# A delta-rule attention with a feed-forward layer: units of four batches, O on four corners, and the first chunk's inverse in halves

## The chip, the cores and the metric

The kernel runs on one core of a Trainium2 chip. The metric is device time in microseconds. Five engines work beside one another, each through its own instructions in order: TensorE (PE; its weight loads are listed as PEld), VectorE (DVE), ScalarE (ACT), GpSimd (POOL) and SyncE (SP), which here issues nearly all DMAs. The kernel before took 265.98 us, the median of three runs (265.12 to 269.84).

## The reference: what is computed

There are 4 batches, 8 heads, 768 tokens and 48 elements per head. For each batch and head, with k normalised:

```
for t in range(S):
    y[:, :, t] = q[t] @ state
    v_old = k_n[t] @ state
    state = state + beta[t] * outer(k_n[t], v[t] - v_old)
```

y is put together as x (3072 tokens by 384), and the feed-forward layer gives `gelu_tanh(x @ w_in) @ w_out`, with w_in 384x2048 and w_out 2048x384. All inputs and the output are float32; the products are made in bf16.

## The kernel before

**Chunks and units.** The 768 tokens are cut into 12 chunks of 64. One chunk of all 32 (batch, head) pairs is two *units* (u = 2c + x). The 128 partitions hold two halves a of 64 tokens. The loads (L458) put batches 2a + x, x = 0 and 1, side by side into the free dimension of half a. Unit x is batch x of each half, with all 8 heads. A head has a slot 2g + p; p says in which 64 rows of the transposed k and q it lies, and g is one of four.

**What a unit does (`prep`).** k is normalised (`sq`, `sum`, `pow`, `eps`, `inv`, then `kn`, L510), times -beta (`kb`, L512), q is copied (`qb`). The twelve 128x128 pieces of k, kb and q are transposed: for units 0 to 5 on PE (`T`, L520, evicted as `kT`), from unit 6 on by a DMA that SP issues (`turn`, L523). `G2` (L542) and `G` (L534) are the products of k with kb, and of kb with k and q; DVE copies them under triangular masks (`ln`, L546; `wp`, L552). A 64x64 triangular inverse per head follows, five rounds of two products with an eviction after each: A, then `rt` on DVE (2 times the identity is added), then B, then `xi` or `bde` on ACT or DVE. For units 0 and 1 the products are on 64x64 corners of the array (`At`, `Bt`, L567), for later ones on block-diagonal 128x128 weights (L596), which POOL and ACT fill.

**What a chunk does (`chain`).** With the state: K (L642) and `R` (subtract v), `U` or `Um` (the inverse applied, L665) and `Un`, S (L675) and `Sn` (the next state), Q (also L642) and O (L689) into one pair of PSUM banks, `On` copies that out into `xo`. In K, Q and S the four 64x64 corners of the array are taken in turn. In O the row half and the column half are the same a, so two corners are used:

```
for p in range(2):
    for a in range(2):
        ins = e.matmul(at("O", P, hf(a), p, x, g), wp[ss[x]][hf(a), 4 * p + g, C:2 * C], ub[hf(a), x, p, g, :], ...)
```

`xo` is transposed to xT: chunks 0, 1 and 11 on PE (`X`, L710, evicted as `xT`), the others by a DMA (`turnx`, L702).

**The feed-forward part (`mlp`).** For one chunk (256 rows): 16 `up` steps of three products (L731), `gelu` on ACT, two blocks of four `down` steps (L743), `Z` (eviction) and the stores (L754), two per block, one for each half a. w_in and w_out are loaded by POOL (`w1`, L466; `w2`, L470).

**The order.** The order on every engine is written out by hand in `ORDER`, and the PSUM bank of every product in `BANKS`; waits follow from the data and the banks. An item such as `up.3.5/0` is the first `up` at position 3.5. `fill` (L428) is a product of zeros that PE runs while it would wait otherwise; there are 71. On SP the order has loads, `turn`, `turnx` and stores in one queue, so that an item that waits holds those behind it.

Of the kernel before, what the change touches and what calls it, by code (L numbers as in the profile page):

```python
# [18 lines left out]
        fill/0 fill/1 fill/2 fill/3 fill/4 fill/5 fill/6 fill/7 fill/8 fill/9 fill/10 fill/11 fill/12 fill/13 fill/14 betaT.-28/0  # L19
        fill/15 fill/16 fill/17 fill/18 fill/19 fill/20 fill/21 fill/22 fill/23 fill/24 fill/25 T.0/0 fill/26 fill/27 T.1/0 G2.0/0  # L20
        G.0/0 fill/28 fill/29 fill/30 fill/31 fill/32 G2.1/0 G.1/0 At.0/0 fill/33 fill/34 fill/35 fill/36 Bt.0/0 fill/37 At.1/0
        fill/38 At.0/1 fill/39 Bt.1/0 fill/40 Bt.0/1 fill/41 fill/42 At.1/1 fill/43 At.0/2 fill/44 Bt.1/1 fill/45 Bt.0/2 fill/46
        At.1/2 At.0/3 T.2/0 Bt.0/3 T.3/0 Bt.1/2 At.0/4 G2.2/0 fill/47 fill/48 G.2/0 G2.3/0 At.1/3 fill/49 fill/50 fill/51 Bt.1/3
        fill/52 fill/53 fill/54 fill/55 At.1/4 Bt.0/4 fill/56 Bt.1/4 fill/57 A.2/0 G.3/0 fill/58 fill/59 B.2/0 U.0.5/0 T.4/0 fill/60
        fill/61 O.0.7/0 A.2/1 G.4/0 fill/62 fill/63 X.0.8/0 B.2/1 A.3/0 fill/64 fill/65 fill/66 up.3.5/0 A.2/2 B.3/0 up.3.5/1 B.2/2
        up.3.5/2 fill/67 up.3.5/3 up.3.25/0 A.3/1 S.0.5/0 up.3.25/1 B.3/1 up.3.25/2 K.2.5/0 up.3.25/3 up.3/0 fill/68 up.3/1 A16.2/0
        G2.4/0 up.3/2 A.3/2 up.3/3 B.2/3 up.3.75/0 fill/69 up.3.75/1 B.3/2 up.3.75/2 A.4/0 up.3.75/3 A16.3/0 fill/70 B.4/0 A32.2/0
        B.3/3 T.5/0 A.4/1 B.2/4 down.4.5/0 B.4/1 down.4.54/0 A32.3/0 down.4.58/0 B.3/4 down.4.62/0 A.4/2 Um.2.5/0 G2.5/0 G.5/0 Q.2.6/0
        S.2.5/0 O.2.7/0 down.4/0 B.4/2 down.4.04/0 A.5/0 down.4.08/0 X.2.8/0 B.5/0 down.4.12/0 up.5.75/0 up.5.25/0 A.5/1 up.5.25/1
        A16.4/0 up.5.25/2 B.5/1 up.5.75/1 up.5.25/3 up.5.75/2 A.5/2 up.5.75/3 K.4.5/0 up.5/0 B.4/3 B.5/2 up.5/1 G2.6/0 G.6/0 up.5/2  # L30
        A32.4/0 up.5.5/0 up.5/3 up.5.5/1 up.5.5/2 A16.5/0 up.5.5/3 B.4/4 A.6/0 B.5/3 down.6.5/0 B.6/0 down.6.54/0 A32.5/0 G2.8/0
        G2.7/0 A.6/1 B.5/4 down.6.58/0 G.8/0 down.6.62/0 Um.4.5/0 B.6/1 Q.4.6/0 G.7/0 O.4.7/0 G2.9/0 A.6/2 A.8/0 down.6/0 A.7/0 B.6/2
        G.9/0 B.8/0 down.6.04/0 B.7/0 down.6.08/0 A.9/0 A16.6/0 A.8/1 down.6.12/0 A.7/1 B.9/0 B.8/1 up.7.25/0 B.7/1 up.7.25/1 B.6/3
        up.7/0 up.7.25/2 up.7/1 up.7.25/3 A32.6/0 up.7/2 A.7/2 up.7/3 A.9/1 A.8/2 S.4.5/0 up.7.5/0 B.9/1 up.7.5/1 B.7/2 up.7.75/0
        up.7.5/2 up.7.75/1 up.7.5/3 up.7.75/2 A16.7/0 up.7.75/3 A.9/2 K.6.5/0 B.7/3 B.6/4 B.8/2 B.9/2 down.8/0 A32.7/0 down.8.04/0
        B.7/4 down.8.08/0 A16.8/0 down.8.12/0 Um.6.5/0 B.8/3 Q.6.6/0 G2.10/0 O.6.7/0 G.10/0 A16.9/0 down.8.5/0 G2.11/0 S.6.5/0 G.11/0
        down.8.54/0 down.8.58/0 B.9/3 A32.8/0 A.10/0 down.8.62/0 K.8.5/0 B.10/0 B.8/4 up.9.75/0 up.9.25/0 up.9.75/1 up.9.25/1
        up.9.75/2 A.10/1 up.9.75/3 A32.9/0 up.9.25/2 A.11/0 B.10/1 up.9.25/3 up.9.5/0 B.9/4 up.9.5/1 G2.13/0 up.9.5/2 up.9.5/3 G.13/0
        Um.8.5/0 Q.8.6/0 B.11/0 A.10/2 G.12/0 G2.12/0 O.8.7/0 A.13/0 B.10/2 up.9/0 up.9/1 B.13/0 A.11/1 up.9/2 A16.10/0 up.9/3 A.12/0
        B.11/1 A.13/1 S.8.5/0 B.10/3 B.13/1 B.12/0 A.11/2 down.10/0 A.12/1 down.10.04/0 B.11/2 down.10.08/0 up.11.75/0 B.12/1  # L40
        up.11.75/1 A.13/2 up.11.75/2 up.11/0 up.11.75/3 B.13/2 up.11/1 A.12/2 A32.10/0 up.11/2 up.11.25/0 up.11/3 up.11.25/1 A16.11/0
        up.11.25/2 B.12/2 up.11.25/3 up.11.5/0 B.11/3 down.10.12/0 up.11.5/1 K.10.5/0 B.10/4 up.11.5/2 A32.11/0 A16.13/0 up.11.5/3
        down.10.5/0 B.11/4 A16.12/0 down.10.54/0 B.13/3 B.12/3 down.10.58/0 Um.10.5/0 down.10.62/0 G2.14/0 Q.10.6/0 S.10.5/0 O.10.7/0
        G.14/0 A32.13/0 down.12/0 A32.12/0 down.12.5/0 B.13/4 down.12.04/0 A.14/0 down.12.08/0 G2.15/0 G.15/0 K.12.5/0 down.12.54/0
        B.12/4 down.12.12/0 B.14/0 down.12.58/0 Um.12.5/0 down.12.62/0 up.13.75/0 Q.12.6/0 G2.17/0 O.12.7/0 G.17/0 up.13.75/1 A.15/0
        up.13.75/2 up.13/0 A.14/1 up.13/1 up.13.75/3 up.13/2 up.13.5/0 up.13/3 up.13.5/1 B.15/0 up.13.5/2 B.14/1 up.13.5/3 up.13.25/0
        G.16/0 G2.16/0 up.13.25/1 up.15.5/0 up.13.25/2 S.12.5/0 up.13.25/3 up.15.5/1 A.15/1 up.15.5/2 A.16/0 A.14/2 up.15.5/3 A.17/0
        B.15/1 down.14/0 B.16/0 B.14/2 down.14.04/0 B.17/0 A.16/1 down.14.08/0 A.15/2 down.14.12/0 A.17/1 B.16/1 up.15/0 B.15/2
        up.15/1 B.17/1 up.15/2 A16.14/0 A16.15/0 up.15/3 up.15.25/0 A.16/2 up.15.25/1 B.14/3 up.15.25/2 A.17/2 up.15.25/3 B.15/3
        B.16/2 K.14.5/0 A32.14/0 up.15.75/0 B.17/2 up.15.75/1 G2.18/0 up.15.75/2 A16.16/0 up.15.75/3 A32.15/0 A16.17/0 B.14/4 B.16/3  # L50
        B.15/4 down.16/0 G.18/0 G2.19/0 down.14.5/0 Um.14.5/0 down.14.54/0 B.17/3 down.16.04/0 S.14.5/0 G.19/0 Q.14.6/0 down.14.58/0
        down.16.08/0 A.19/0 A.18/0 O.14.7/0 K.16.5/0 down.14.62/0 A32.17/0 B.18/0 B.19/0 down.16.12/0 down.16.5/0 B.17/4 A.18/1
        A32.16/0 down.16.54/0 A.19/1 down.16.58/0 B.18/1 G2.20/0 G.20/0 B.16/4 down.16.62/0 up.17.5/0 B.19/1 up.17.5/1 Um.16.5/0
        up.17.5/2 A.20/0 up.17.5/3 up.17.75/0 G2.21/0 up.17.75/1 B.20/0 up.17.75/2 up.17.25/0 up.17.75/3 up.17.25/1 A.19/2 up.17.25/2
# [12 lines left out]
        up.25.25/3 down.24.04/0 down.24.5/0 down.24.08/0 up.25/0 up.25.5/0 up.25/1 down.24.12/0 up.25/2 down.24.54/0 up.25/3
        down.24.58/0 up.25.5/1 down.24.62/0 down.26/0 up.25.5/2 down.26.5/0 up.25.5/3 down.26.54/0 down.26.04/0 down.26.58/0
        down.26.08/0 down.26.62/0 down.26.12/0
    """,  # L70
    "act": """
        loadk.-40/0 tmpl.-11/0 beta.-24.5/0 pow.0/0 triw.-3/0 ladj16.-0.2/0 ladj16.0.8/0 pow.1/0 tri.-5/0 ladj32.0.8/0 tri.-7/0
# [237 lines left out]
def bass_deltanet__then__act_gelu_tanh_kernel(  # L310
# [13 lines left out]
    NU = 2 * NC  # L324
    DIRECT = lambda u: (2, 3, 4, 5) if u < 8 else (2, 4)
    GROUPS = [[c] for c in range(NC)]
    TURN, TURNX, TILED = 6, 2, 2

    F = Flow()
    A = F.add  # L330

    with nc.allow_non_contiguous_dma("strided loads"), nc.allow_low_precision("bf16 pipeline"):
# [39 lines left out]
        def hf(a, n=C):  # L372
            return slice(64 * a, 64 * a + n)
# [437 lines left out]
```

## Time and profile before

| | |
|---|---|
| median of three runs | 265.98 us (265.12 to 269.84) |
| profiled execution | 266.2 us |
| its span in the profile | 264.4 us |
| clock granted to PE | 1.00 |
| chain that ended last | PE 78%, DVE 7%, DMA 5%, rest under 3% each |
| first product of the feed-forward part | starts at 39.35 us |
| last product of PE | ends at about 260.6 us |
| last O | starts at 238.54 us |

The profile is of one execution. A group line gives the source line, the engine, the operation, out<-in with shapes, the count, the busy time, the mean duration of one, and the engine's idle time before it with what ended it. Instructions of one engine overlap, so that the time from the start of one to the start of the next is often less than its duration.

### The profile page before, as it was taken

The numbers are of one execution on the slowest core, as the hardware profiler recorded it, in microseconds if no ns is written. First come the engines' busy times: TensorE is split into PE (matmuls) and PEld (weight loads), VectorE is DVE, ScalarE is ACT, GpSimd is POOL, SyncE is SP. The second block draws the span as 40 slices with busy tenths as digits, with TensorE's granted clock in tenths as the row PEclk, the third lists the DMA queues.
The fourth block names the chain that finished last, engine by engine and source line by source line (L and its number), as shares of the span: only waits on it lengthen the run. The fifth ranks groups of instructions, "written<-read, shape, count | busy, mean of one in ns | idle before, by whom it ended". The sixth has DMA issues, their size and how long they took to land.

```text
span 264.4 us, 12466 instructions
## 1 busy us (share of the span) xinstructions
PE 253.8 (96%) x5629; PEld 191.6 (72%) x5629; DVE 202.0 (76%) x317; ACT 174.8 (66%) x264; POOL 144.5 (55%) x220
## 2 busy tenths in 40 slices
PE   7899998999899999999999999999999999999994
PEld 2557566877677876877886888877888878778762
DVE  8899796978899999899779888889886876551000
ACT  3758676777886894498663468935788657556431
POOL 8633698849899889875855674480635222110000
PEclk9999999999999999999999999999999999999999
DMA  5996999999999999948997589238149064044023
GB/s 105 175 154 124 146 204 193 177 134 151 158 164 155 141 162 137 188 88 165 169 173 100 125 165 147 48 81 144 25 63 180 5 133 82 2 35 101 6 47 72
DMA packets 117908, 31.86 MB, mean 120 GB/s; under 512 B 111968, under 2 KB 117088, under 8 KB 117856
## 3 DMA queue, kind: packets, MB, share of 16 engines
q1 hardware_dynamic: 113968, 27.63, 69.7%
q0 software_dynamic: 2880, 3.15, 7.6%
q8 instruction: 44, 0.72, 1.2%
q10 hardware_dynamic: 1008, 0.30, 0.5%
q14 instruction: 8, 0.07, 0.1%
HBM read 20.64 MB, written 4.72 MB: 96 GB/s over the span
## 4 chain that ended last, share of the span: by engine, by line
PE 78%; DVE 7%; DMA 5%; ACT 2%; SPq 2%; issue 2%; POOL 2%; POOLq 0%; ACTq 0%
PE ps L743 23%; PE ps L731 21%; PE ps L596 18%; DMA W<-in_moe_w_in_dram 4%; PE ps L428 3%; PE ps L567 3%; PE ps L642 2%; DMA kraw<-in_k_dram 2%; DVE ln L546 2%; PE ps L689 2%; SPq L523 2%; PE ps L534 2%; PE ps L665 1%; DVE rt L603 1%; PE ps L542 1%
## 5 line engine op out<-in xcount | busy, mean ns | idle before, releaser
L731 PE MATMUL ps<-xT,W 128*128 128x256 bf16 x576 | 82.4, 273 | 0.8 <-DMA W<-in_moe_w_in_dram 0.7
L376 ACT ACTIVATE bd<-ps 64x512 bf16<-64x512 f32 x111 | 64.5, 589 | 18.0 <-PE ps L596 16.0
L743 PE MATMUL ps<-W,gT 128*128 128x384 bf16 x384 | 76.3, 326 | 0.0
L736 ACT ACTIVATE gT<-ps 128x1024 bf16<-128x1024 f32 x48 | 48.4, 1021 | 27.0 <-PE ps L731 26.6
L731 PEld LDWEIGHTS ps<-xT,W 128*128 128x128 bf16 x576 | 48.7, 98 | 9.5 <-DMA W<-in_moe_w_in_dram 1.0
L603 DVE TENSOR_TENSOR rt<-ps,two 128x512 bf16<-128x512 f32 x66 | 44.2, 687 | 10.6 <-PE ps L596 9.9
L590 POOL COPY bd<-xi 64x256 f32<-64x256 f32 x64 | 25.1, 394 | 42.4 <-ACT xi L376 30.2
L743 PEld LDWEIGHTS ps<-W,gT 128*128 128x128 bf16 x384 | 32.3, 97 | 15.0 <-ACT gT L736 0.2
L586 POOL TENSOR_SCALAR_AFFINE_SELECT bd<-ln 64x512 bf16<-64x512 bf16 x44 | 28.9, 658 | 22.5 <-DVE ln L546 18.4
L376 DVE CAST bd<-ps 64x512 bf16<-64x512 f32 x45 | 30.8, 686 | 5.1 <-PE ps L596 3.9
L552 DVE CAST_PREDICATED wp<-mup,ps 128x1024 bf16<-128x1024 uint16 (+1 forms) x26 | 29.3, 1133 | 2.3 <-PE ps L534 2.3
L489 POOL TENSOR_TENSOR nrm<-nrm,half 128x16 f32<-128x16 f32 x9 | 26.3, 2929 | 2.1 <-DVE nrm L486 1.9
L376 ACT ACTIVATE xi<-ps 128x512 bf16<-128x512 f32 x31 | 18.3, 594 | 12.1 <-PE ps L596 6.9
L596 PE MATMUL ps<-rt,bd 128*128 128x64 bf16 x528 | 25.5, 194 | 0.3 <-DVE rt L603 0.2
L596 PE MATMUL ps<-wp,bd 128*128 128x64 bf16 (+1 forms) x528 | 24.7, 188 | 1.0 <-issue 0.5
L596 PEld LDWEIGHTS ps<-wp,bd 128*128 128x128 bf16 x528 | 21.3, 97 | 5.5 <-issue 1.1
L596 PEld LDWEIGHTS ps<-rt,bd 128*128 128x128 bf16 x528 | 21.1, 98 | 5.0 <-DVE rt L603 2.4
L603 DVE TENSOR_TENSOR rl<-ps,two 128x384 bf16<-128x384 f32 (+1 forms) x44 | 20.8, 485 | 4.8 <-PE ps L596 4.4
L428 PE MATMUL ps<-wz 128*128 128x512 bf16 x71 | 21.8, 413 | 1.3 <-DVE wz L382 1.2
L510 POOL TENSOR_TENSOR tok<-kraw,nrm 128x384 bf16<-128x384 f32 x21 | 17.6, 841 | 8.4 <-DVE nrm L493 8.1
L546 DVE CAST_PREDICATED ln<-mlo,ps 128x512 bf16<-128x512 uint16 x24 | 16.5, 687 | 4.9 <-PE ps L542 4.6
L512 POOL TENSOR_TENSOR tok<-tok,bsb 128x384 bf16<-128x384 bf16 x21 | 17.5, 836 | 2.7 <-DVE tok L510 1.9
(98 smaller groups left out, 334.5 us busy)
## 6 DMA issues: line engine op xcount, KB each, us to landing
qraw<-in_q_dram SPq DMA_DIRECT2D x24, 192.0 KB, 5.1
vraw<-in_v_dram SPq DMA_DIRECT2D x24, 192.0 KB, 4.9
out_dram<-ob SPq DMA_DIRECT2D x47, 96.0 KB, 2.6
kraw<-in_k_dram SPq DMA_DIRECT2D x22, 192.0 KB, 5.3
W<-in_moe_w_in_dram POOLq DMA_DIRECT2D x2, 768.0 KB, 9.2
W<-in_moe_w_out_dram POOLq DMA_DIRECT2D x2, 768.0 KB, 10.8
kraw<-in_k_dram SPq DMA_DIRECT2D x3, 96.0 KB, 4.0
kT<-tok SPq DMA_TRANSPOSE x18, 5.0
```

Of the source, the lines that this page charges most:

```text
L376: return e.activation(out, in_, ACT.Copy) if e is nc.scalar else e.tensor_copy(out, in_)
L428: return e.matmul(P(f"fill{i}")[:, :], wz[:, 0:128], wz[:, 0:512])
L489: e.tensor_tensor(nr[:, 1, hx], nr[:, 0, hx], half[:, hx], ALU.pow),
L546: A("dve", z + "ln", lambda e, P: e.copy_predicated(ln[m][:, :, :].rearrange("p (x g) t -> p x g t", x=2), mlo[:, :].bitcast(U16).unsqueez ...
L552: A("dve", z + ("wp" if nh == 2 else "wph"), lambda e, P, cs=cs, nh=nh: e.copy_predicated(wp[s][:, :, cs], mup[:, cs].bitcast(U16).unsquee ...
L586: A("pool", z + "X1", lambda e, P, src=src, dst=dst: e.affine_select(out=dst, in_=src, compare_op=ALU.not_equal, fill=1.0, base=0, pattern ...
L590: A("pool", z + "bdc", lambda e, P, src=src, dst=dst: e.tensor_copy(dst.bitcast(F32), src.bitcast(F32)), reads=[w("xi")], writes=[n(f"bd{a ...
L596: ins = e.matmul(P(name)[:, C * h + lo:C * h + C], bd[s][:, h, :], rhs[:, h, lo:C])
L603: A("dve", z + f"rt{lo or str()}", lambda e, P, i=i, lo=lo, r_=r_: e.tensor_tensor(r_[:, :, lo:C], P(ps(f"A{i}")).rearrange("p (h t) -> p ...
L731: ins = e.matmul(P(ph)[:, w * f:w * f + w].rearrange("p (x t) -> p x t", x=2), W1[:, j, 128 * (i + f):128 * (i + f) + 128], x_[:, :, j, :] ...
L736: A("act", z + "gelu", lambda e, P, i=i, ph=ph: e.activation(g_[:, i:i + nf, 0:w], P(ph).rearrange("p (f t) -> p f t", f=nf), ACT.Gelu_app ...
L743: ins = e.matmul(P(po)[:, 0:DM], g_[:, f, 128 * b:128 * b + 128], W2[:, f, :], start=(f == 0), stop=(f == FC - 1))
```

## The change

**Layout.** The loads put batches 2a + p side by side, and unit x takes every second of the 16 columns (p, head): the heads 2g + x of all four batches. p, which was the parity of the head, is now the batch within the half. The state, `rs` and `xo` are ordered g before x, so that the 384 columns of a token are consecutive; `R` and `On` copy without a permutation.

**O and Q.** Both write PSUM rows of half a ^ p in place of a, so that O's four products per g are on four corners. A token's half in `xo` is then a ^ p. For block 0 (p = 0) the halves are in order and both are stored by one DMA (`outw`); block 1 has two stores with the halves exchanged.

**First chunk.** For units 0 and 1 the inverse is made for four head slots at a time (`Ath`, `Bth`, `rth`, `xih`; five rounds as before). Transposes and G of q are split off (`Tq`, `Gh`, evicted by `qT`, `wph`), so that k goes ahead. U, O, X and their evictions of chunk 0 are done for each unit (x) by itself, X for each block.

**Other.** Chunk 1's xT is made by a DMA (`TURNX` 1 in place of 2). The table of the square root is loaded at ACT's start (`tmpl` waits for it). `ORDER` and `BANKS` are new throughout: 68 `fill` in place of 71; on SP the first `turnx` stands after chunk 5's k loads and ahead of one q load, chunk 2's v loads and the `turn` of units 7 and 8.

The core of the diff:

```diff
-    TURN, TURNX, TILED = 6, 2, 2
+    TURN, TURNX, TILED, SPLIT = 6, 1, 2, 2
...
-                view = {"k": k, "q": q, "v": v}[n].rearrange("(a x) h (c t) d -> a c t (x h) d", a=2, t=C)
+                view = {"k": k, "q": q, "v": v}[n].rearrange("(a p) h (c t) d -> a c t (p h) d", a=2, t=C)
...
-            kr, qr = (raw[y][r][:, H * x:H * x + H, :] for y in "kq")
+            kr, qr = (raw[y][r][:, x::2, :].rearrange("t (p g) d -> t p g d", p=2) for y in "kq")
...
+                for ys, tn in (((0, 1), "T"), ((2,), "Tq")) if u < SPLIT else (((0, 1, 2), "T"),):
...
+            for gn, rhs in (("G", (0,)), ("Gq", (2,))) if u < SPLIT else (("G", (0, 2)),):
...
+                        A("pe", z + "Ath", lambda e, P, pa=pa, con=con, lo=lo, f=product: f(e, P, pa, con, lo), ...
+                          alloc=(pa, 1), mode="t", mm=H, pos=u)
+                        A("dve", z + f"rt{lo or str()}h", lambda e, P, pa=pa, lo=lo, r_=r_, y=y: e.tensor_tensor(
+                            r_[:, hs[y], lo:C], P(pa)[:, 0:4 * C].rearrange("p (h t) -> p h t", h=4)[:, :, lo:C],
...
-                o = 512 * b + 4 * D * x + D * g
-                return P(ps(name))[r, o:o + D]
+                o = 512 * b + 2 * D * g + D * x
+                return P(ps(name) if name != "O" or not first else ps(f"O{x}"))[r, o:o + D]
...
-                        ins = e.matmul(at(name, P, hf(a), p, x, g), kT[ss[x]][hf(p, D), y, g, hf(a)], so[hf(p, D), a, x, g, :],
+                        ins = e.matmul(at(name, P, hf(a ^ p if y else a), p, x, g), kT[ss[x]][hf(p, D), y, g, hf(a)], so[hf(p, D), a, g, x, :],
...
-                    for p in range(2):
-                        for a in range(2):
-                            ins = e.matmul(at("O", P, hf(a), p, x, g), wp[ss[x]][hf(a), 4 * p + g, C:2 * C], ub[hf(a), x, p, g, :],
+                    for p, a in quad if x in xs else ():
+                        ins = e.matmul(at("O", P, hf(a ^ p), p, x, g), wp[ss[x]][hf(a), 4 * p + g, C:2 * C], ub[hf(a), x, p, g, :],
...
-                for a in range(2):
-                    r0 = (2 * a + b % 2) * S + C * g[b // 2]
-                    A("act" if final and a else "sp", z + "out", lambda e, P, a=a, r0=r0, o_=o_: e.dma_start(out[r0:r0 + C, :], o_[hf(a), :]),
+                rows = out.rearrange("(a p c t) m -> p c a t m", a=2, p=2, t=C)[b % 2, g[b // 2]]
+                for a in (0, 1) if b % 2 else (slice(0, 2),):
```

More of the change, by code (lines that the diff above doesn't have):

```diff
@@ L149 @@
+        out.26.5/0 outw.26/0
     """,
@@ L410, in preset @@
                 A("pool", "0tmplz", lambda e, P: e.memset(tmpl[:, C:2 * C], 0.0), writes=["tmplz"], pos=-11)
-                A("act", "0tmpl", lambda e, P: e.activation(tmpl[:, 0:C], two[:, :], ACT.Copy, scale=-0.5), reads=["two"],
+                A("act", "0tmpl", lambda e, P: e.activation(tmpl[:, 0:C], two[:, :], ACT.Copy, scale=-0.5), reads=["two", "one"],
                   writes=["tmpl"], pos=-11)
@@ L561, in prep @@
+            if u < TILED:
+                hs = [slice(4 * y, 4 * y + 4) for y in range(2)]
+                for y, _, k_ in halves:
+                    A(("dve", "pool"), z + "X1h", lambda e, P, y=y: e.tensor_tensor(
+                        xi[m][:, hs[y], :], ln[m][:, hs[y], :], two[:, :].unsqueeze(1).to_broadcast([128, 4, C]), ALU.add), reads=[w("ln") + k_, w("ln"), "two"],
+                      writes=[w("xi") + k_], pos=u)
                 for i in range(1, 6):
                     con, conn = (wp[s][:, :, 0:C], n("wp")) if i % 2 else (ln[m], w("ln"))
[L564 to L568 removed]
@@ L720, in mlp @@
             w = 256 * len(g)
[L721 removed]
+            x_, xn = xT[gi % NX], [f"xT{gi % NX}.{256 * i}{k_}" for i in range(len(g)) for k_ in "ab"]
             g_, gn = gT[gi % NG], f"gT{gi % NG}"
```

456 lines of the change are left out of this document (244 added, 212 removed), and 17 rows, old and new, of the table BANKS.

## The prediction

> **What bounds the kernel now.** I read the page's busy shares and clock first, then the busy times by stretch, then TensorE's groups by form, and last the timeline around the first chunk.
>
> ```profile
> PE 253.8 (96%) x5629; PEld 191.6 (72%) x5629; DVE 202.0 (76%) x317; ACT 174.8 (66%) x264; POOL 144.5 (55%) x220
> ...
> PEclk9999999999999999999999999999999999999999
> ```
>
> TensorE (PE) is busy 96% of the span at full clock. No other engine comes near that on average, but the stretches say more (columns: stretch, length, then PE, PEld, DVE, ACT, POOL, clock, DMA share, GB/s):
>
> ```profile
> 30.00:40.00 10.00, 9.94 (x231) 6.41 (x230) 8.53 (x12) 7.11 (x12) 8.77 (x10) 1.00 1.09 186
> ...
> 60.00:80.00 20.00, 18.93 (x458) 14.59 (x455) 18.01 (x30) 16.27 (x25) 18.02 (x19) 1.00 1.22 159
> 80.00:100.00 20.00, 19.78 (x416) 15.86 (x414) 19.25 (x30) 16.37 (x27) 17.86 (x20) 1.00 1.16 146
> 100.00:120.00 20.00, 19.07 (x562) 15.24 (x560) 18.54 (x30) 12.95 (x20) 16.12 (x27) 1.00 0.94 142
> ...
> 140.00:160.00 20.00, 20.00 (x463) 15.38 (x460) 17.72 (x24) 10.23 (x15) 12.11 (x21) 1.00 0.85 142
> ```
>
> From 60 us on PE misses only 1 us in 20, and from 140 us nothing: an instruction less on PE there ends the kernel earlier, as long as its order always has something ready. DVE and POOL are nearly as full between 60 and 120 us. Before 40 us "busy" misleads, because PE runs fillers (products of zeros, L428) while it waits:
>
> ```profile
> L428 PE MATMUL ps<-wz 128*128 128x512 bf16 x71 | 21.8, 413 | 1.3 <-DVE wz L382 1.2
> ...
> L642 PE MATMUL ps<-st,kT 48*64 48x48 bf16 x704 | 9.7, 189 | 0.0
> ...
> L689 PE MATMUL ps<-us,wp 64*64 64x48 bf16 x384 | 8.3, 187 | 0.3
> ...
> L675 PE MATMUL ps<-us,tok 64*64 64x48 bf16 x352 | 4.8, 188 | 0.2 <-ACT us L376 0.2
> ```
>
> Of the 71 fillers 67 start before 39.35 us, where the first product of the feed-forward part (`up`, L731) starts. The other three groups have 48 columns each and one instruction lasts 187 to 189 ns in all of them, but 32 of L689 (the O step) take 8.3/12 = 0.69 us and 32 of L675 (the S step) 4.8/11 = 0.44 us. The timeline shows the same:
>
> ```profile
> 15.43 0.44 PE L567 MATMUL ps<-wp,xi 64*64 64x64 bf16 x16 [0.25 <-POOL xi L558]
> ...
> 35.88 0.69 PE L689 MATMUL ps<-us,wp 64*64 64x48 bf16 x32
> ...
> 39.35 0.24 PEld L731 LDWEIGHTS ps<-xT,W 128*128 128x128 bf16 x3 [0.53 <-issue]
> ...
> 43.59 0.44 PE L675 MATMUL ps<-us,tok 64*64 64x48 bf16 x32
> ```
>
> Start to start that is (0.69-0.19)/31 = 16 ns for O and 8 ns for S. O uses two corners of the array (row half a with column half a), S and the K and Q products (L642) use four. L567, on two corners with 64 columns, also shows 16 ns: about 33 ns for a corner in every case.
>
> **The change, part by part.**
>
> *O on four corners.* Same 32 instructions. Nearest rows: L675 on four corners below (0.44 us), L689 itself above (0.69 us). I take 0.44, since L642 and L675, with different row orders, both give it: 0.25 us for each O, 11 of them in the stretch that PE bounds: -2.75 us (bounds 0 and -2.75). The twelfth lies in the head and is counted there. Q stays on four corners: 0. What becomes late instead: nothing, O ends in an eviction (On) that only gains from an earlier start.
>
> What speaks against it: in K and S each row half keeps a bank of its own, in the new O both row halves write both banks, and no row has that on four corners. The nearest is L567, whose two row halves write one bank: its products start 16 ns apart, while 64 columns take 27 ns (three of L731's 256 columns take 0.33 us). They overlap in the shared bank.
>
> The Trainium skill, page "TensorEngine Tiling (Array Packing)", section "Gotcha 1: PSUM Pressure", says that different row tiles cannot access one PSUM bank at the same time. By that rule the new O would stay at 0.69 us, and the sum would be -1.05 in place of -3.8 us. The trace does not agree with it, by the 16 ns against 27 ns of L567.
>
> *The head.* I add up what PE must issue before the first `up`, by its order. Prices from rows: filler 0.214 us (0.427 for the first ones), twelve transposes 0.67, G2 0.22, G 0.27, an A or B product of a unit 0.235, one of the first two units 0.33, U 0.58, O 0.58 or 0.3, X 0.33. Before: 15 fillers end at 6.48 us; then beta's transposes 0.86, 52 fillers 11.1, five T 3.35, four G2 0.88, five G 1.35, twenty At and Bt 6.6, five A or B 1.2, U, O and X 1.5: 33.3 us. It starts at 39.35, so 6.0 us are gaps: 0.66 for beta and 5.4 beside 22 runs of fillers, 0.245 each. After: ten fillers end at 5.5; beta 0.86, 51 fillers 10.9, transposes 3.35, G2 0.9, G in parts 1.4, forty half products 6.8, seven A or B 1.65, U, O, X 1.2: 32.6. With 0.245 for each of 17 runs and 0.5 for beta the first `up` starts at 37.3: -2.05 us. Then PE is also two A or B products ahead and one G behind (-0.2), but seven fillers follow in place of four (+0.64), in six runs in place of four (+0.5). Head: -1.1 us. Two causes carry it. ScalarE's second table load (1.28 us at 5.93, ahead of the first square root, in the chain) moves to the start, beside the k load (`tmpl` now waits for it too, but the triangles made from it are wanted only at 13 us); and the first transposes wait no longer for q. Beta's load stands second on both queues. On DVE and ACT a 512-column step of 0.69 us becomes two of about 0.42 (the 256-column row), 0.33 start to start against 0.60 for one: 0.07 us more for each pair, on engines that wait, but a half can go on while the other is computed. Bounds: +0.6 (the overlap brings nothing, the later fillers stay) and -3.3 (below). W1's first half is loaded by POOL behind the same steps; PE waited 0.72 us for it at 42.9, and I leave that as it is.
>
> *Chunk 1's X by DMA.* Six transposes leave PE (-0.33) and an eviction of 0.56 us leaves DVE. The DMA lands in 3.1 us (2.7 to 4.6 for xT), after On's 0.81. Between O and the first `up` of that chunk the new order has two fillers, S, four `down` of 0.65 and five A or B, 4.6 us: hidden up to 3.7 us, 0.9 us late at worst. But SP's queue gets one more item ahead of one q load, two v loads and the kT transposes of units 7 and 8, while SP issues without a pause. If On ends at 57.5, the transpose issues until 59.6 and the loads until 62; unit 7's transpose (2.15 us to issue, 5.0 to landing) lands at 67.2, unit 8's at 69.5. PE asks for them at about 67.9 and 68.9: +0.4 us taken, bounds 0 and +5.8 (the slowest rows, below).
>
> *Stores.* One 192 KB DMA in place of two of 96 KB for every first block: 12 issues of 0.6 us less on SP. None is on PE's path, and the last stores are as before: 0. They ease SP from 78 us on, where the first store was issued; if they went slower nothing waits before the end.
>
> *New layout.* The loads keep their shape (192-byte pieces). The steps kn, kb and qb read runs of 48 at twice the stride; 64x256 strided copies cost POOL 394 ns and 128x512 contiguous ones 847, so no price per element shows: 0, bounds 0 and +5 us on POOL for 60 to 100 us (half of the 10.2 us of these steps there, against 4.1 us that POOL idles). R and On become contiguous copies of the same size: 0.
>
> Sum: -1.1 - 2.75 - 0.33 + 0.4 = -3.8 us. The profiled execution took 266.2 us with a span of 264.4; 1.8 us around it stay. 266.2 - 3.8 = 262.4; against the median of 265.98 that is **262.2 us**.
>
> **Rivals.** (1) *O gains nothing.* The two row halves wait for one another in the shared banks. For it: no row has four corners with shared banks. Against: L567 shares one and overlaps. -3.8 + 2.75: 264.9 us. The page named above would have it so.
>
> (2) *The halves hide more.* Followed along data instead of PE's order: the last rt32 ended at 31.8 and `up` came 7.55 us later. With kn 1.5 us earlier and the first product 2.5 us earlier (13.0 against 15.43), the last rt32 at 30.7, and half steps for U, On and xT, the data are there at 36.0: -3.3 instead of -2.05. If the gaps beside the later fillers also vanish: -3.3 - 0.2 + 0.64 - 2.75 - 0.33 + 0.4 = -5.5, 260.4 us. Against: PE's order puts T, A and B ahead of `up`, and DVE has 71 steps up to the last rt32 where it had 54.
>
> (3) *Slower: SP's queue.* Place: the kT transposes of units 7 and 8. If each takes the longest issue (4.56 us) and landing (8.1), unit 8's lands at 74.7, not 69.5, and PE stops 5.8 us at its G: 268.0 us; if units 9 and 10 repeat it, 273.8. It decides from 3.8 us past PE's need. For it: DMA shares above 1.1 until 100 us, and PE waited 0.61 us for kT already. Against: the queue had the same number of items by then.
>
> **How the numbers follow.** Forecast 0.38, rival (1) 0.13, (2) 0.34, (3) 0.15. Over 2%, about what a measurement of this kernel can tell from no change, means below 260.7 or above 271.3. Faster: all but 0.01 of (2) and the forecast's lower edge, 0.05: 0.38. Slower: 0.14 of (3). Same: 0.48. The range reaches from rival (2) without the later fillers, the wait for kT and the one for W1 (-0.64 - 0.4 - 0.72: 258.7) to (1) with 2.6 us of (3) (267.5); most of (3) lies outside. The forecast's own range is 260.5 to 264.
>
> **What would show it.** Right: O groups of 32 in 0.44 us; the first `up` near 37.3; PE busy from 60 us as before; no wait for kT over 1 us. Wrong: O at 0.69; `up` not before 39; a wait of PE for a DMA between 60 and 80 us; POOL's kn above 0.9 us; DVE late in 60 to 120 us.

## The result, and the profile after

The changed kernel took **276.15 us** (median of 4 runs, 274.36 to 277.47), beside 265.74 us for the kernel before on the same chip: a ratio of 1.040 (95% interval 1.031 to 1.048). The prediction was 262.2 us, range 258.7 to 267.5. It was wrong by 13.95 us, and in its sign. The profiled execution took 277.13 us with a span of 275.4.

Three things changed in the profile. First the end. The stretches of the changed kernel behind TensorE's last product (columns: stretch, length, PE, PEld, DVE, ACT, POOL, clock, DMA share, GB/s):

```profile
264.00:266.00 2.00, 1.99 (x13) 0.98 (x10) 0.00 (x0) 0.49 (x1) 0.00 (x0) 1.00 0.33 41
266.00:268.00 2.00, 0.00 (x0) 0.00 (x0) 0.56 (x1) 0.00 (x0) 0.00 (x0) 1.00 0.68 134
268.00:270.00 2.00, 0.00 (x0) 0.00 (x0) 0.00 (x0) 0.00 (x0) 0.00 (x0) 1.00 0.36 119
270.00:272.00 2.00, 0.00 (x0) 0.00 (x0) 0.00 (x0) 0.00 (x0) 0.00 (x0) 0.79 0.13 40
272.00:274.00 2.00, 0.00 (x0) 0.00 (x0) 0.00 (x0) 0.00 (x0) 0.00 (x0) 0.50 0.13 51
```

and of the kernel before:

```profile
260.00:262.00 2.00, 0.54 (x4) 0.10 (x1) 0.00 (x0) 0.91 (x2) 0.00 (x0) 1.00 0.22 45
262.00:264.00 2.00, 0.00 (x0) 0.00 (x0) 0.00 (x0) 0.00 (x0) 0.00 (x0) 1.00 0.59 151
```

Before, the span ends 3.8 us after the last product, with a DMA share of 0.59. After, it ends 9.4 us after it, and for four of these the share is 0.13: 0.13 x 16 is as much as two DMA engines that are busy without a pause, at 40 to 51 GB/s. The only transfers left then are stores. That is 5.6 of the 11.0 us by which the span grew.

Second, waits of TensorE for DMAs that it did not have before. TensorE's timeline of the changed kernel (start, duration, in brackets the idle time before it and what ended it):

```profile
64.28 1.16 PE L775 MATMUL ps<-xT,W 128*128 128x256 bf16 x9 [0.44 <-DMA xT<-xo]
...
111.24 2.72 PE L775 MATMUL ps<-xT,W 128*128 128x256 bf16 x12 [3.09 <-DMA xT<-xo]
...
160.82 1.14 PE L775 MATMUL ps<-xT,W 128*128 128x256 bf16 x9 [1.73 <-DMA xT<-xo]
```

The first of these waits, at 64.28 us, comes before any store: the first one is issued at 88.75 us.

```profile
88.75 0.67 SPq L798 DMA_DIRECT2D out_dram<-ob  x1
```

It is a wait for chunk 1's xT, which the change makes by a DMA and no longer on TensorE. The chain of waits of the changed kernel goes through the other two:

```profile
92.59 9.25 DMA kT<-tok
...
104.33 6.78 DMA xT<-xo
...
152.73 7.96 DMA xT<-xo
```

The long wait costs more than its 3.09 us. The clock falls behind it (same columns as above):

```profile
105.00:110.00 5.00, 3.15 (x90) 1.96 (x88) 4.75 (x7) 0.60 (x2) 4.66 (x7) 1.00 1.05 116
110.00:115.00 5.00, 3.76 (x36) 2.93 (x37) 0.79 (x2) 0.41 (x1) 2.60 (x4) 0.66 1.08 192
```

A clock of 0.66 over five microseconds is 1.7 us of full speed lost (0.34 x 5).

Third, the parts that the prediction spoke of. O's group now reads as foreseen, 5.3/12 = 0.44 us for 32:

```profile
L720 PE MATMUL ps<-us,wp 64*64 64x48 bf16 x384 | 5.3, 188 | 0.0
```

In the head the first product of the inverse starts at 12.55 us (15.43 before), yet the first `up` starts at 40.22 (39.38), not at 37.3. The stretches of the changed kernel there:

```profile
10.00:20.00 10.00, 9.22 (x246) 5.63 (x247) 9.52 (x25) 8.15 (x18) 7.82 (x12) 1.00 1.28 159
20.00:30.00 10.00, 7.75 (x218) 5.50 (x222) 9.05 (x22) 7.58 (x14) 4.00 (x6) 1.00 1.02 149
30.00:40.00 10.00, 8.12 (x221) 5.95 (x224) 9.51 (x19) 6.14 (x14) 9.58 (x10) 1.00 1.09 187
```

DVE is busy 9.5, 9.1 and 9.5 of 10 us (8.8, 8.6 and 8.5 before), and TensorE, fillers included, only 7.75 and 8.12 in the last two (9.43 and 9.94 before). TensorE's issue is not what sets this stretch any more.

### The profile page after: what moved, and what is told of

The parts are those of the page before. It is cut to its first block, busy times and chain, and to the rows that moved or that the text cites. A ratio compares the mean times of both kernels' runs of the same rounds, so it can differ in the third digit from the quotient of the medians.

```text
span 275.4 us, 12507 instructions
## 1 busy us (share of the span) xinstructions
PE 250.3 (91%) x5640; PEld 190.0 (69%) x5652; DVE 203.7 (74%) x336; ACT 176.6 (64%) x273; POOL 143.3 (52%) x221
## 4 chain that ended last, share of the span: by engine, by line
PE 65%; DMA 16%; DVE 6%; POOL 3%; ACT 3%; issue 2%; SPq 1%; ACTq 0%; POOLq 0%; DVEq 0%
PE ps L787 19%; PE ps L775 18%; PE ps L620 14%; DMA kT<-tok 6%; DMA xT<-xo 5%; DMA qraw<-in_q_dram 3%; PE ps L433 2%; PE ps L592 2%; PE ps L665 2%; PE ps L544 1%; DMA braw<-in_beta_dram 1%; PE ps L552 1%; DVE wp L574 1%; PE ps L524 1%; PE ps L698 1%
## 5 line engine op out<-in xcount | busy, mean ns | idle before, releaser
L775 PE MATMUL ps<-xT,W 128*128 128x256 bf16 x576 | 84.3, 276 | 5.5 <-DMA xT<-xo 5.3
L381 ACT ACTIVATE bd<-ps 64x512 bf16<-64x512 f32 x114 | 66.5, 590 | 18.3 <-PE ps L620 16.3
L775 PEld LDWEIGHTS ps<-xT,W 128*128 128x128 bf16 x576 | 49.1, 99 | 14.3 <-issue 5.4
L614 POOL COPY bd<-xi 64x256 f32<-64x256 f32 x64 | 25.1, 395 | 40.6 <-ACT xi L381 28.3
L381 DVE CAST bd<-ps 64x512 bf16<-64x512 f32 x42 | 28.8, 687 | 5.4 <-PE ps L620 4.6
L574 DVE CAST_PREDICATED wp<-mup,ps 128x1024 bf16<-128x1024 uint16 x22 | 26.7, 1218 | 2.9 <-PE ps L544 2.8
L620 PEld LDWEIGHTS ps<-rt,bd 128*128 128x128 bf16 x528 | 21.8, 98 | 5.3 <-DVE rt L627 1.7
L381 ACT ACTIVATE xi<-ps 128x512 bf16<-128x512 f32 (+1 forms) x35 | 17.6, 516 | 10.2 <-PE ps L592 4.9
L514 POOL TENSOR_TENSOR tok<-kraw,nrm 128x384 bf16<-128x384 f32 x22 | 18.2, 833 | 6.5 <-DVE nrm L497 6.1
L559 DVE CAST_PREDICATED ln<-mlo,ps 128x512 bf16<-128x512 uint16 (+1 forms) x26 | 16.6, 643 | 4.5 <-PE ps L552 4.1
L433 PE MATMUL ps<-wz 128*128 128x512 bf16 x56 | 16.9, 418 | 2.1 <-DVE wz L387 1.2
```

What stands on the lines that cost most here:

```text
L381: return e.activation(out, in_, ACT.Copy) if e is nc.scalar else e.tensor_copy(out, in_)
L433: return e.matmul(P(f"fill{i}")[:, :], wz[:, 0:128], wz[:, 0:512])
L514: A("dve" if u < 2 else POOL, z + "kn", lambda e, P: e.tensor_tensor(kn, kr, nr[:, 3, hx].rearrange("t (p g) -> t p g", p=2).unsqueeze(3). ...
L574: A("dve", z + "wp", lambda e, P: e.copy_predicated(wp[s][:, :, :], mup[:, :].bitcast(U16).unsqueeze(1).to_broadcast([128, H, 2 * C]), P(p ...
L614: A("pool", z + "bdc", lambda e, P, src=src, dst=dst: e.tensor_copy(dst.bitcast(F32), src.bitcast(F32)), reads=[w("xi")], writes=[n(f"bd{a ...
L620: ins = e.matmul(P(name)[:, C * h + lo:C * h + C], bd[s][:, h, :], rhs[:, h, lo:C])
```

## Experiments

**The theory after the result.** The joined store is slow because its access pattern has an outermost dimension of 2, the two halves a: it occupies two DMA engines, ends late, and holds up the transposes that share them. Rivals: the new order loads SP's queue at another place; the 192 KB of one DMA matter, not its pattern; the head.

### The joined store, three ways

*e1_split*: the changed kernel, with block 0's store as two DMAs again.

```diff
-                for a in (0, 1) if b % 2 else (slice(0, 2),):
+                for a in (0, 1):
...
-                        rows[a ^ 1] if b % 2 else rows, o_[hf(a), :] if b % 2 else o_[:, :]),
+                        rows[a ^ 1] if b % 2 else rows[a], o_[hf(a), :]),
```

> The changed kernel with the first block's store made by two DMAs of 64 rows again, at the same place of the queue. Theory A (the joined store, whose outermost dimension has two entries, runs on two of the sixteen DMA engines, lands late and holds up the transposes behind it): the end after PE's last product falls from 9.4 to about 4 us, the waits of PE for xT and kT past 60 us (some 7 us with the slow clock after them) fall below 2 us: 263 to 266 us. Theory B (the new order, SP's queue above all, is late by itself): only the end gets shorter, 270 to 271 us. Theory C (the number of stores is what matters, fewer are better): slower than 276.

Measured: 266.07 us (10 runs), ratio 0.997 (0.992 to 1.001). TensorE's last product ends 5.5 us earlier than in the changed kernel, and the span 4.0 us after it, with a DMA share of 0.55 up to the end:

```profile
260.00:262.00 2.00, 0.44 (x3) 0.05 (x1) 0.56 (x1) 0.32 (x1) 0.00 (x0) 1.00 0.60 128
262.00:264.00 2.00, 0.00 (x0) 0.00 (x0) 0.00 (x0) 0.00 (x0) 0.00 (x0) 0.85 0.55 144
```

The three waits for xT above are gone.

*e2_before_joined*: the kernel before, with block 0's stores joined as in the change (at the place of the earlier one in SP's queue) and nothing else.

```diff
-                for a in range(2):
-                    r0 = (2 * a + b % 2) * S + C * g[b // 2]
...
+                rows = out.rearrange("(a p c t) m -> p c a t m", a=2, p=2, t=C)[b % 2, g[b // 2]]
+                for a in (0, 1) if b % 2 else (slice(0, 2),):
...
```

> The kernel before with the two stores of each first block joined into one DMA of 2 x 64 rows, at the place of the earlier of them; nothing else. Theory A: the end after PE's last product grows by 4 to 6 us, xT transposes land later than 4.6 us, some wait of PE for them: 270 to 276 us. Theory B and C: 264 to 267 us.

Measured: 272.24 us beside 265.9, ratio 1.024 (1.016 to 1.032). Its end is that of the changed kernel in small, and the transposes of xo begin to be waited for (0.20, 0.87 us):

```profile
264.00:266.00 2.00, 0.00 (x0) 0.00 (x0) 0.00 (x0) 0.00 (x0) 0.00 (x0) 1.00 0.17 46
266.00:268.00 2.00, 0.00 (x0) 0.00 (x0) 0.00 (x0) 0.00 (x0) 0.00 (x0) 0.57 0.13 44
268.00:269.90 1.90, 0.00 (x0) 0.00 (x0) 0.00 (x0) 0.00 (x0) 0.00 (x0) 0.50 0.07 25
```

*e3_one_run*: the changed kernel, with the joined store going to 128 consecutive rows of the output in place of two runs of 64. The rows of the output are exchanged by this.

```diff
+                at0 = 128 * (g[b // 2] % 6) + 2 * S * (g[b // 2] // 6)
...
-                        rows[a ^ 1] if b % 2 else rows, o_[hf(a), :] if b % 2 else o_[:, :]),
+                        rows[a ^ 1] if b % 2 else out[at0:at0 + 128, :], o_[hf(a), :] if b % 2 else o_[:, :]),
```

> The changed kernel with each first block still stored by one DMA of 192 KB, but into 128 consecutive rows of the output (for chunks 0 to 11 in turn in the rows of batches 0 and 2), so that its access pattern has 128 entries and not 2 x 64; rows of the output are exchanged, the amount is the same. Theory A: the store uses all sixteen DMA engines, and the time is that of the kernel with split stores, 263 to 266 us. If 192 KB in one DMA are slow by themselves: near 276 us.

Measured: 264.48 us, ratio 0.995 (0.991 to 1.000). The same 12 DMAs of 192 KB now land in 3.2 us (the last column: KB each, median us to landing):

```profile
out_dram<-ob SPq DMA_DIRECT2D x12, 192.0 KB, 3.2
out_dram<-ob SPq DMA_DIRECT2D x23, 96.0 KB, 2.9
```

What follows: the joined store is the loss, by its pattern and not by its size or its place in SP's queue. Undoing it gives back 276.15 - 266.07 = 10.1 us; by the ratios, each to the kernel before as it was measured beside it, it is (1.040 - 0.997) x 266 = 11.4 us. In the kernel before it costs 6.3 us. How the store delays the transposes is argued and not shown: the trace does not name the DMA engine of a transfer. The Trainium skill, page "DMA: Bandwidth & Descriptors", section "Why a DMA increments its semaphore by 16 and not by 1", says that the number of engines is the largest up to 16 that divides the slowest dimension of both access patterns. By that rule the 2 x 64 x 384 pattern gets two engines and the 128 x 384 pattern 16. The trace agrees: share 0.13 for the one, 3.2 us for the other.

### O and the layout, alone

*e4_before_O4* is the kernel before with O and Q on half a ^ p and O's four corners in turn (the output's tokens are exchanged). *e7_before_layout_O4* adds the layout and stores the rows in their places; the order of all engines is that of before.

```diff
-                        ins = e.matmul(at(name, P, hf(a), p, x, g), ...
+                        ins = e.matmul(at(name, P, hf(a ^ p if y else a), p, x, g), ...
...
-                    for p in range(2):
-                        for a in range(2):
-                            ins = e.matmul(at("O", P, hf(a), p, x, g), ...
+                    for a in range(2):
+                        for p in range(2):
+                            ins = e.matmul(at("O", P, hf(a ^ p), p, x, g), ...
```

> The kernel before with Q's and O's output rows on half a ^ p and O's products in the order that takes four corners in turn; layout, loads and stores as before, so that for one of the two blocks tokens are exchanged between batches in the output. If O's 0.25 us are on the path that sets the end: 12 x 0.25 = 3 us less, 262.5 to 263.5 us, and 32 O in 0.44 us. If PE's time is refilled by other waits: 265 to 266 us.

> The kernel before with its own order, two stores per block and X of chunk 1 on PE; only the layout (units of four batches) and O and Q on half a^p are taken from the change. The output is the reference's. If the layout costs nothing: as e4_before_O4 (264.9 us), 264.2 to 265.6, O groups of 32 in 0.44 us or less, POOL's kn as long as in the kernel before. Rival (reading runs of 48 at twice the stride slows POOL and DVE): kn above 0.9 us, waits of PE for kT or POOL between 60 and 120 us, and 267 us or more.

Measured: 264.91 us (ratio 0.994, 0.990 to 0.998) and 264.68 us beside 266.57 (0.994, 0.991 to 0.998). The groups of e7, O first, then kn on POOL:

```profile
L688 PE MATMUL ps<-us,wp 64*64 64x48 bf16 x384 | 5.6, 189 | 0.4
...
L510 POOL TENSOR_TENSOR tok<-kraw,nrm 128x384 bf16<-128x384 f32 x21 | 17.4, 832 | 8.9 <-DVE nrm L493 8.6
```

and kn in the kernel before:

```profile
L510 POOL TENSOR_TENSOR tok<-kraw,nrm 128x384 bf16<-128x384 f32 x21 | 17.6, 841 | 8.4 <-DVE nrm L493 8.1
```

The layout costs POOL nothing (832 and 841 ns). O falls by (8.3 - 5.6)/12 = 0.22 us each, but the time by 0.0056 x 266 = 1.5 us (0.5 to 2.4 by the interval), about half of the 2.75. The traces show one place where a lead is lost. The first `up` starts 0.5 us (e4) and 0.65 us (e7) earlier than before, but at 42.9 us all three kernels wait for W1, for 0.72 us before, 1.21 in e4 and 1.30 in e7, and leave that wait within 0.13 us of one another. From there to the start of the last O it is 195.6 us before, 194.6 in e4 and 194.8 in e7: ten O's brought 0.8 to 1.0 us, where ten times 0.22 is 2.2. TensorE reads as full there (20.00 of 20 in most stretches), so the profile does not show where the rest was given back; this stays open. e7 has the lowest ratio of the kernels here with the reference's output; e1_split's interval (0.992 to 1.001) overlaps its own.

### The head: halves or whole units

*e6_whole_units* is e1_split with the ten half steps per unit merged to five; *e11_whole_units_filled* adds fillers (products of zeros) at the pause that e6 turned out to have.

```diff
-            halves = [(y, slice(y, y + 1), "ab"[y]) for y in range(2)]
+            halves = [(0, slice(0, 2), "a")]
...
-                hs = [slice(4 * y, 4 * y + 4) for y in range(2)]
+                hs = [slice(0, 8)]
```

> The changed kernel with block 0's store split into two (as in e1_split), and the first chunk's inverse in whole units again: each pair of half products, of half additions and of half evictions of units 0 and 1 is one step over eight head slots, at the later place of the two, its eviction on ScalarE where one of the two was there. Theory (DVE is the bound of the head, and the halves cost it): in e1_split DVE has gaps of only 3.5 us between 12 and 34 us; seven half evictions of 0.33 us and 0.07 us for each of nine merged additions leave it, so the first `up` starts 1 to 2 us earlier than 41.2, at 39.2 to 40.2, and the time is 264 to 265.3 us. Rival (the halves help, because each half goes on while the other is computed): the first `up` starts at 42 or later and the time is 267 us or more.

> e6_whole_units (the changed kernel, split stores, the first chunk's inverse in whole units) with seven more fillers at 23.6 us, and the two behind them in a bank that waits for no eviction, where e6 had a pause of TensorE of 1.64 us and then a clock of 0.50 for 3.4 us. Theory (the halves cost DVE more than they hide): the clock stays at 1.00, the first `up` starts at 40.3 to 41.0 where e1_split has 41.2, and the time is 0.3 to 1 us below e1_split's ratio of 0.9966, at 0.993 to 0.996. Rival (halves are a gain): the first `up` at 41.5 or later without a slow clock, ratio 0.998 or more.

Measured: e6 267.01 us, ratio 1.003 (0.999 to 1.007), first `up` at 42.1. Both theories missed the reason, a pause in e6:

```profile
25.70 0.91 PE L431 MATMUL ps<-wz 128*128 128x512 bf16 x2 [1.64 <-ACT kT L379]
...
26.00:27.00 1.00, 1.00 (x20) 0.46 (x20) 0.49 (x1) 1.00 (x2) 0.00 (x0) 0.50 1.27 132
```

The filler waits for a bank that ScalarE frees, and the clock then reads 0.50 for 3.4 us. e11, without the pause, has its first `up` at 41.2, just e1_split's 41.2, and 268.11 us (1.005, 1.002 to 1.009). So the halves neither lengthen nor shorten the head by as much as a microsecond, and the theory that halving costs the head is not borne out. In time whole units are even slower than e1_split (0.997, 0.992 to 1.001). In e11's profile that lies behind the first `up`: TensorE waits for chunk 1's xT,

```profile
67.48 1.16 PE L774 MATMUL ps<-xT,W 128*128 128x256 bf16 x9 [2.54 <-DMA xT<-xo]
```

and for 1.85 us at 109.14, after which the clock reads 0.50 for 3.4 us. This is one execution; whether the whole units cause it is not shown.

### The head: DVE's share

*e9_dve_dose* adds two of the memsets below to DVE; *e12_short_sums* takes 2.2 us from it.

```diff
+            A("dve", "1dose", lambda e, P: e.memset(junk[:, :], 0.0), writes=["junk"], pos=3)
```

```diff
-... e.tensor_reduce(nr[:, 0, hx], sqx, AX.X, ALU.add),
+... e.tensor_reduce(nr[:, 0, hx], sqx if c in (0,) or c > 3 else sqx[:, :, 0:6], AX.X, ALU.add),
```

> e1_split with two extra memsets of DVE (scratch, 0.41 us start to start each, 0.82 together) ahead of the second additions of the first chunk, at about 16 us; nothing reads them. Theory (DVE bounds the head): nearly all of it arrives, the first `up` starts 0.6 to 0.9 us later than in e1_split (41.2), at 41.8 to 42.1, and the time rises by as much. Rival (DVE waits there as the prediction said, for PE or data): the first `up` within 0.2 us of 41.2.

> e1_split in which DVE's sums of squares for chunks 1 to 3 run over 6 of the 48 elements (the norm is scaled up; this part of the computation is changed): three steps of 0.94 us ahead of the first `up` become about 0.2 us each, 2.2 us less of DVE, with the order as it is. Theory (DVE's fixed work is what stretches the head; it has 1.3 us of gaps between 13.6 and 31.6 us in the changed kernel): the first `up` starts 0.8 to 2 us earlier than in e1_split, at 39.2 to 40.4. Rival (each half waits for its data, and DVE only fills the time): the first `up` within 0.4 us of 41.2.

Measured: e9 269.78 us (1.011, 1.006 to 1.016), first `up` at 43.1. That looks like the dose and more, but the first product already starts at 14.65 (12.62 in e1_split): the ten fillers ahead of the first transposes took 3.89 us in that execution and 2.33 in e1_split, before any dose. From the first product on it is 28.5 us in e9 and 28.6 in e1_split. The dose did not arrive. By the ratios e9 takes 3.9 us more than e1_split; 2 us are this late start in the profiled execution, the rest is not explained. e12: 267.42 us (1.002, 0.999 to 1.006), first `up` at 41.6, with a clock of 0.91 from 25 to 30 us and 0.75 from 30 to 35 (1.7 us lost). Without that loss it would be at 39.9 (an estimate, 41.6 - 1.7); as measured, nothing was gained. DVE as the bound of the head is not borne out by e9 and undecided by e12.

### The head: the table load

*e8_table_first* and *e10_table_first_beta* are e7 with ScalarE's square-root table load first; in e10 beta's load is issued ahead of it, and DVE's `one` ahead of `pad`.

```diff
-        loadk.-40/0 tmpl.-11/0 beta.-24.5/0 pow.0/0 ... tri.-3/0 tabS.-30/0
+        loadk.-40/0 beta.-24.5/0 tabS.-30/0 tmpl.-11/0 pow.0/0 ... tri.-3/0
```

> e7_before_layout_O4 with one item moved: ScalarE's square-root table load (1.28 us) stands at its start and no longer ahead of the first square root. Theory: the first product of the inverse starts 1.3 us earlier than in e7 (15.4 to 14.1); DVE has gaps there in the order of before (2.8 us between 12 and 34 us), so 0.5 to 1.3 us of it reach the first `up`, and the time falls by as much against e7. Rival (fixed work of DVE sets the first `up`, as in the changed kernel): the first `up` within 0.3 us of e7's, and no gain.

> e7_before_layout_O4 with the square-root table load at ScalarE's start as in e8_table_first, but with beta's second load issued ahead of it (in e8 it went behind, landed late, TensorE stood still for 2.0 us and its clock read 0.50 from 9 to 15 us). Theory: the clock stays at 1.00, the first product of the inverse comes 0.5 to 1.3 us earlier than in e7 (14.9), the first `up` 0.3 to 1 us earlier than 38.7, and the time is 263.5 to 264.6 us where e7 is 264.7. Rival (other fixed work sets the head, or W1's load sets the first `up`): first `up` at 38.5 to 39, time as e7.

Measured: e8 267.67 us, ratio 1.004 (1.001 to 1.008). Beta's load went behind `tmpl`, TensorE stood still, and the clock read 0.50 from 9.0 to 15.8 us:

```profile
7.00:8.00 1.00, 0.00 (x0) 0.00 (x0) 1.00 (x4) 0.87 (x4) 0.87 (x3) 1.00 1.40 197
8.00:9.00 1.00, 0.27 (x4) 0.27 (x5) 0.83 (x3) 1.00 (x4) 0.94 (x2) 1.00 1.47 161
9.00:10.00 1.00, 1.00 (x12) 0.94 (x11) 0.00 (x0) 0.68 (x2) 0.45 (x1) 0.50 1.44 167
```

The first `up` came at 42.7, 4 us late. e10: 266.2 us (0.999, 0.994 to 1.003), no pause at 7 us, yet the first transposes at 10.54 (10.26 in e7), the first product at 15.32 (14.86) and the first `up` at 40.16 (38.73), later than either theory had it; TensorE paused for 1.42 us at 20.58 on the way. In the order of before 26 fillers and beta's transposes stand ahead of the first transposes and end at about 10.4 us whatever ScalarE does. So far the rival held: the table load is worth nothing there. By this reading, what brought the changed kernel's first product forward is the 20 fillers in place of 26, with the table load making it possible; no run has the one without the other.

### The head: two places in the new order

e1_split, once with unit 3's transposes evicted by DVE and not by ScalarE (*e13*), once with the A product that waits 1.02 us ahead of the first `up` moved behind the second `up` (*e14*), and with both (*e15*). The diff has the orders of ScalarE, DVE and TensorE.

```diff
-        sq.4/0 kT.2/0 kT.3/0 pow.4/0
+        sq.4/0 kT.2/0 pow.4/0
...
-        xih.0/4 rth.1/4
+        xih.0/4 kT.3/0 rth.1/4
...
-        A.2/2 up.3.5/0 A.3/1 up.3.5/1 B.2/2
+        up.3.5/0 A.3/1 up.3.5/1 A.2/2 B.2/2
```

> e1_split with the eviction of unit 3's transposes (1.45 us on ScalarE, 0.96 on DVE) moved from ScalarE to DVE, behind two half evictions of the inverse, about where the kernel before has it. Theory (in the new order two such evictions stand back to back on ScalarE, 2.7 us, and hold the inverse's evictions that come next): ScalarE's three evictions at 26.07 start about 1.2 us earlier, and 0.5 to 1.2 us of it arrive at the first `up` (40.0 to 40.7). Rival (DVE is as full, and pays 0.96 for 1.45): first `up` at 41.0 to 41.8.

> e1_split with one A product of unit 2, that waits 1.02 us for ScalarE directly ahead of the first `up`, moved behind the second `up`. Theory (this wait holds `up`, whose data have been there): the first `up` starts 0.8 to 1.2 us earlier than 41.2, at 40.0 to 40.4, and 0 to 1 us of it reach the end, 265 to 266 us. Rival (`up` waits for its own data or for W1 there): first `up` within 0.3 us of 41.2.

> Both moves of e13_kT3_on_dve and e14_A2_behind_up in e1_split. If the two are the places that hold the head: first `up` at 39.0 to 40.0, and 264 to 265.3 us, ratio 0.991 to 0.995. If either theory falls: no earlier than the better one of the two alone.

> The kernel of e13_kT3_on_dve, profiled again. Measured as the distance from the start of the first product to the start of the first `up`: 28.6 us in e1_split. If ScalarE's two evictions back to back hold the head: 26.8 to 28.0 us. If not: 28.3 or more.

> The kernel of e14_A2_behind_up, profiled again. The same distance (28.6 us in e1_split): 27.4 to 27.8 if the wait of 1.02 us ahead of `up` is all that this move takes away; 28.3 or more if `up` waits for its own data there; less than 27 would show that the product's place also held other work.

Measured: e13 266.95 us (1.000, 0.996 to 1.005), e14 265.94 (1.000, 0.996 to 1.003), e15 265.74 (0.998, 0.995 to 1.002). e13's first profile is of an execution of 471.82 us, with products twice as long throughout (a product of 256 columns every 0.222 us, 0.109 in the others); it is not in the table. The profiles in one table (us; the start of the first and of the last group of products of the first chunk's inverse, the first `up`, and the two distances):

| kernel | first | last | `up` | first to last | last to `up` |
|---|---|---|---|---|---|
| before | 15.43 | 31.86 | 39.38 | 16.4 | 7.5 |
| after | 12.55 | 32.72 | 40.22 | 20.2 | 7.5 |
| e1_split | 12.62 | 33.80 | 41.22 | 21.2 | 7.4 |
| e7 (order of before) | 14.86 | 31.00 | 38.73 | 16.1 | 7.7 |
| e11 (whole units) | 12.90 | 33.43 | 41.18 | 20.5 | 7.8 |
| e13, profiled again | 12.47 | 33.31 | 40.82 | 20.8 | 7.5 |
| e14 (clock 0.50 from 30.4 to 33.9) | 14.40 | 36.66 | 42.65 | 22.3 | 6.0 |
| e14, profiled again | 12.61 | 32.78 | 38.86 | 20.2 | 6.1 |
| e15 | 14.58 | 34.09 | 40.18 | 19.5 | 6.1 |

ScalarE's two evictions are not the place (first product to `up`: 28.35 us, where 28.3 or more was to mean no). The product ahead of `up` is one: the last stretch falls by 1.3 to 1.4 us in all three profiles that have the move. The second profile of e14 has its first `up` 2.4 us earlier than e1_split; 1.0 us of that lies ahead of the last product of the inverse, where the two orders are the same, and is scatter. In the times nothing larger than their intervals is left of it, and e15's first `up` (40.18) and time missed their forecast.

Why the ten rounds take 19.5 to 21.2 us in the new order, in halves or whole, where the old one takes 16.4, can be read in part. The stretch from the first to the last product of the inverse, before and after (columns as above):

```profile
15.43:32.10 16.67, 16.07 (x415) 10.16 (x416) 14.29 (x26) 12.04 (x22) 7.19 (x9) 1.00 0.95 137
```

```profile
12.55:32.84 20.29, 17.36 (x499) 12.01 (x506) 18.87 (x48) 14.34 (x29) 12.67 (x18) 1.00 1.08 151
```

More other work lies in it. Besides fillers and the 320 products of the inverse, TensorE runs 72 products there before and 160 after (transposes, G2, G, the first A and B of unit 2), and DVE is busy 14.3 us before and 18.9 us after, of 20.3. How much of the 3.8 us each costs is not settled: e9 gave DVE more, e11 gave it less (16.7 of 20.8 us), and neither moved the stretch by as much as a microsecond.

## Why the prediction was wrong, step by step

**Stores, put at 0: the step that failed.** The text said that "none is on PE's path, and the last stores are as before: 0", and "if they went slower nothing waits before the end". All three parts fell. The last joined store is at the end, and the span ends 5.6 us later behind TensorE's last product. SP's transposes behind such a store land later: xT's median rose from 3.1 to 4.1 us (below, before and after), its longest from 4.6 to 8.0, and TensorE waited for it.

```profile
xT<-xo SPq DMA_TRANSPOSE x9, 3.1
```

```profile
xT<-xo SPq DMA_TRANSPOSE x10, 4.1
```

And the longest wait pulled the clock down. Measured: +10.1 us (e1_split), where the prediction counted 12 issues saved and did not look at the shape of the new access pattern. In the old DMAs the slowest dimension was 64; joining made it 2.

**O on four corners, -2.75: right in mechanism, half in size.** 0.44 us for 32, as the row of S said. The rule that two row halves cannot use one bank at a time, which rival (1) stood on, does not hold here: both halves write both banks, each time the other column half, at 8 ns start to start. But e4 and e7 gained 1.5 us. That 0.25 us off TensorE's issue ends the kernel 0.25 us earlier was assumed from its 20.00 of 20; ten O's brought 0.8 to 1.0 us.

**Head, -1.1: wrong in sign.** The first product came forward by 2.9 us, more than forecast (13.0 was named; 12.55 measured). But the chunk needs both units, and the second one gained little. The normalised k of unit 1, before and after:

```profile
10.43 0.55 DVE L510 TENSOR_TENSOR tok<-kraw,nrm 128x384 bf16<-128x384 f32 x1
```

```profile
10.12 0.55 DVE L514 TENSOR_TENSOR tok<-kraw,nrm 128x384 bf16<-128x384 f32 x1
```

Only 0.31 us, where rival (2) took 1.5 for both; unit 1's first product went from 17.46 to 15.74. The rounds then took 3.8 us longer, and `up` came 0.8 us later, not 2.05 earlier. Adding up what TensorE issues, with 0.245 us for each run of fillers, treats the pauses as constant. They were not: TensorE is busy 1.7 us less in 20 to 30 us and 1.8 us less in 30 to 40 us.

**SP's queue, +0.4 and rival (3).** The place was near, the cause was not. kT was waited for 0.56 us at 80.08, not 5.8; the waits that mattered were for xT at 111 and 161 us. With the stores split (e1_split) the two later waits for xT are gone, so the new queue order was not their cause. Rival (3) had 15% and a price of 268 to 273.8; the outcome lies above it, for another reason.

**Chunk 1's X by DMA and the layout.** The layout: 0, shown by e7 (832 and 841 ns). X by DMA was not tried by itself, and it was not as well hidden as the text had it ("0.9 us late at worst", with a landing in 3.1 us). Chunk 1's xT landed 4.9 us after its issue in the changed kernel, 5.3 in e1_split and 6.0 in e11. TensorE waited 0.44 us for it in the first and 2.54 us in the last, where the stores are split; in e1_split a pause of 1.43 us at 64.32 hid it. All parts without the joined store gave -0.9 us (e1_split, ratio 0.997) where -3.8 was forecast. O accounts for -1.5 (by e7), so head, X and order together gave +0.6 in place of -1.0; the intervals of both ratios are about as wide as this difference.

## What to carry to other kernels

A DMA is priced by its access pattern before its count: here two DMAs of 64 rows beat one of 2 x 64, and one of 128 consecutive rows is as good as the two. An item that "nothing waits for" can still delay transfers that others wait for, so ask what runs beside it, and what the last one does at the end. Where a step needs several inputs, follow the latest of them, not the one that the change brings forward.

## What was not expected of the hardware

- **A short wait of TensorE can cost again what it cost.** After 3.09 us at 108 us the granted clock read 0.50 from 110.7 to 114.1 us; after two microseconds with a wait of 1.64 (e6) 0.50 for 3.4 us; after 2.0 us at 7 to 8.7 us (e8) for 6.8 us. The length of the wait does not decide it. A pause of 1.33 us in e12, at 27.8, was followed by 0.50 for 3.4 us, and one of 1.34 us at the same place in e1_split by no lower clock, nor were waits of 1.73 us (changed kernel, 160.82) and 2.54 us (e11, 67.48). The Trainium skill, page "TensorE: Matmul & The Clock Gate", section "Part 1: The HAM clock gate (the "warmup" mystery)", gives a free-running window of 3413 ns for this. The trace agrees with the 3.4 us at half speed, and 6.8 us is two of them, but the fall came after waits of half such a window.
- **TensorE starts at half speed, for a time that differs between executions.** The ten fillers ahead of the first transposes took 2.33 us in e1_split and 3.89 us in e9. One by one, fillers start 0.43 us apart at first and 0.22 us later; the step comes at about 4 us in e1_split and at 10.4 us in e9 and e15, and everything behind it moves by up to 2 us. That is why the table above has distances. It may be a part of the scatter of the times (e1_split's ten runs lie between 263.6 and 267.9 us); that is not shown.
- **Pauses inside a group.** TensorE stops between two products of one group, with nothing that the profile names as the cause, in most kernels at 27 to 30 us and again at 105 to 110:

```profile
28.65 0.24 PE L544 MATMUL ps<-kT 48*64 48x128 bf16 x2 [1.34 <-issue]
...
107.61 0.26 PE L620 MATMUL ps<-wp,bd 128*128 128x64 bf16 x3 [1.54 <-issue]
```

These are e1_split's; in the changed kernel the first is 0.92 us, in the kernel before both are under 0.6 us. They are as large as the differences that the later experiments looked for, and their cause is open.
